# Block 1 of a chunked linear attention in 64-token chunks, spread between parts of the projection before it

## The chip, the cores and the metric

One Trainium2 chip, one core of it. The metric is the device time of one execution in microseconds; lower is better. The kernel takes float32 inputs and gives float32; inside it works in bf16 with float32 sums.

## The reference

An attention with decay (lightning attention) is followed by a gated feed-forward layer. B = 4 batches, H = 8 heads, S = 768 tokens, D = 64; the model width is 512 and d_ff is 1536.

```python
for b in range(nb):                       # blocks of 64 tokens
    intra = einsum('bhic,bhjc->bhij', qb, kb) * Dmask      # lam ** (i - j), i >= j
    intra = einsum('bhij,bhjd->bhid', intra, vb)
    inter = einsum('bhid,bhde->bhie', qb * lam_pow, kv_state)
    out[:, :, sl] = intra + inter
    kv_state = lam_block * kv_state + einsum('bhsd,bhse->bhde', kb * rev_pow, vb)
...
x = out, as (B * S) x 512
result = (sigmoid(x @ w_gate) * (x @ w_val)) @ w_out
```

The length at which the tokens are cut into pieces is free as long as decays and states follow it: a piece of 128 tokens gives the same result as two of 64.

## The kernel before, in words

The 768 tokens are walked in six blocks n = 0 to 5 of C = 128 tokens, for all 4 batches and 8 heads at once; so a block is 512 rows of the feed-forward layer. For each block there are three stages.

1. Attention. q and k are transposed so that the head dimension lies on the partitions (`QS`, `KS`), two heads on the 128 partitions; q is multiplied by the decay table `lamq`. Scores (`sp`) are masked into `MT`, outputs (`op`) are summed from the state (inter: `ST` times `QS`) and from the scores (intra: `v` times `MT`) and copied to `XT`, and the state of the next block is made (`cp`, from the decayed keys `KD`, then an update into `ST`).
2. `piece_gv` (L566): for each of 12 slices `ft` of d_ff four matmuls with WG into `gp`, four with WV into `vp` (each of 512 columns, in `product`, L556 to L561); ACT makes the tanh of gp (`sg`), DVE multiplies it with vp into `ht`.
3. `piece_po` (L592): for each batch `tt` twelve matmuls with WO into `po`, then a copy to `ob` and a store.

What sets the order is a list, `plan`, written by hand: units of stage 2 or 3, each with work of the next block's attention that is issued right behind it. Every engine does its instructions in the order in which they are issued. [...]

The blocks differ. Block 0 has a form of its own (`t_0`, `s_0`, `a_0`, `c_0`), in which tokens are laid in pairs; TensorE first multiplies zeros (`zeros`, L613) while loads are under way. Blocks from `FIRST_XBAR` = 2 on take q and k transposed by DMA and work in chunks of L = 64 tokens: `chunk_s`, `chunk_m`, `chunk_i`, `chunk_a`, `chunk_x`, `chunk_c`, with matmuls of 64 x 64 that stand four at a time in the quadrants of the array; the state between the two chunks is made by `update_0` (L533, from the decayed state `XD` of `decayed`), the one for the next block by `update_1` (L540). `in_order` (L505) makes TensorE wait until a named matmul has finished[...]; it stands between inter and intra outputs. For half of the batches (2 and 3) heads, and in the chunk form also the halves of the token rows of k and v, are swapped when loaded (`load`, L89).

Block 1 lies between the two. Its q and k are transposed by TensorE (`trans`, L706, `t_`, L280: matmuls of 128 x 128), and it works in one piece of 128 tokens: `piece_s` (L380), `piece_m`, `piece_i` (L398), `piece_a` (L410), `piece_x`, `piece_c` (L433). It needs tables of its own (`block_tables` L249, `block_mask` L262) and `chunk_lamq` (L259), which turns the query table into the chunk form once block 1 is done. In the plan (L763 to L770) its work lies behind parts of block 0's projection `po`, cut into first and second halves of six matmuls: transposes of batches 0 and 1 behind the second unit, their scores behind the third, transposes of batches 2 and 3 behind the sixth, scores behind the seventh, and `att(1)`, that is outputs, XT and states together, behind the last.

```python
order = [(gp, WG, whole), (vp, WV, whole)]
if ft == 0 and n <= 1:
    order = [(gp, WG, first), (vp, WV, first), (gp, WG, second), (vp, WV, second)][1 - n:]
```

These lines (L571 to L573) cut the first unit of blocks 0 and 1 into halves by batches, so that it can begin when XT holds batches 0 and 1.

## Time and profile before

| what | value |
|---|---|
| median of 3 runs | 223.56 us (223.34 to 223.59) |
| the profiled execution's own time | 223.48 us |
| its span, first to last instruction | 221.7 us |
| TensorE matmuls (PE) busy | 214.0 us, 97% |
| VectorE (DVE), ScalarE (ACT) busy | 104.6 us, 107.9 us |
| four matmuls of gp or vp, 512 columns | 0.86 us |
| DVE copy of one bank of XT, block 1 | two in 1.29 us |
| DVE update_0, one bank (L536) | 0.68 us |
| ACT copy of one bank of XT (L510) | 0.60 us |

The page gives each engine's busy time, then the span in 40 slices of 5.5 us with the busy share of each in tenths, then the chain of work that ended last: from the last instruction back to what released it. The timeline lists instructions in order of time, with the idle time of the engine ahead of each and what ended it in brackets. [...]

### The profile page before, as it was taken

How to read it: one execution, taken by the hardware profiler on the slowest of the kernel's cores; microseconds unless marked ns; L12 is line 12 of the kernel's file. 1: busy time of each engine (PE TensorE's matmuls, PEld its weight loads, DVE VectorE, ACT ScalarE, POOL GpSimd, SP SyncE). 2: the span in 40 equal slices, each digit the busy share in tenths (PEclk: the TensorE clock that was granted, in tenths of full speed). 3: DMA queues.
4: the chain of work that ended last, by engine and by line, in shares of the span. 5: the costliest groups of instructions: out<-in, count | busy, mean ns of one | idle time of the engine just before them, and what ended most of it. 6: DMA issues, size and time to landing. Idle time of an engine off the chain costs nothing.

```text
span 221.7 us, 5479 instructions
## 1 busy us (share of the span) xinstructions
PE 214.0 (97%) x2299; PEld 107.5 (48%) x2310; DVE 104.6 (47%) x192; ACT 107.9 (49%) x236; POOL 72.9 (33%) x101
## 2 busy tenths in 40 slices
PE   7689999999999999999999999999999999999994
PEld 2564444557445454454544444544445544444443
DVE  4854575539757430749420659430649400333301
ACT  5748764594393243773433683342592342333221
POOL 7999855760296009800970050000000000000000
PEclk9999999999999999999999999999999999999999
DMA  5999999999999999999999993012100012100022
GB/s 115 176 179 187 195 200 181 168 156 155 152 98 168 236 235 128 176 185 113 88 151 197 234 75 24 3 50 95 47 0 3 3 50 95 47 1 0 3 96 95
DMA packets 99657, 25.27 MB, mean 114 GB/s; under 512 B 90288, under 2 KB 96688, under 8 KB 99632
## 3 DMA queue, kind: packets, MB, share of 16 engines
q0 software_dynamic: 78128, 13.90, 78.3%
q1 hardware_dynamic: 20688, 10.69, 20.0%
q10 hardware_dynamic: 816, 0.33, 0.6%
q8 instruction: 18, 0.29, 0.5%
q14 instruction: 7, 0.06, 0.1%
HBM read 28.32 MB, written 6.29 MB: 156 GB/s over the span
## 4 chain that ended last, share of the span: by engine, by line
PE 92%; POOL 2%; DMA 2%; issue 1%; ACT 1%; POOLq 0%
PE gp L559 28%; PE po L599 28%; PE vp L559 28%; DMA vb<-in_v_dram 2%; PE sp L460 1%; PE op L498 1%; PE op L484 1%; POOL qb L119 1%; PE cp L521 1%; PE op L318 1%; POOL kb L119 1%; PE sp L386 0%; ACT XT L325 0%; PE op L417 0%; PE tq L284 0%
## 5 line engine op out<-in xcount | busy, mean ns | idle before, releaser
L554 DVE SCALAR_TENSOR_TENSOR ht<-sg,vp 128x512 bf16<-128x512 f32 x72 | 49.4, 686 | 84.4 <-PE vp L559 79.0
L559 PE MATMUL gp<-XT,WG 128*128 128x512 bf16 (+1 forms) x296 | 74.3, 373 | 0.5 <-ACT XT L325 0.5
L559 PE MATMUL vp<-XT,WV 128*128 128x512 bf16 (+1 forms) x296 | 74.3, 373 | 0.0
L577 ACT ACTIVATE sg<-gp 128x512 f32<-128x512 f32 x72 | 43.0, 597 | 57.0 <-PE gp L559 57.0
L599 PE MATMUL po<-WO,ht 128*128 128x512 bf16 (+2 forms) x291 | 63.4, 370 | 0.6 <-issue 0.2
L559 PEld LDWEIGHTS <-WV 128*128 128x128 bf16 x296 | 28.9, 98 | 33.3
L559 PEld LDWEIGHTS <-WG 128*128 128x128 bf16 x296 | 28.6, 98 | 32.6 <-issue 0.5
L599 PEld LDWEIGHTS <-ht 128*128 128x128 bf16 x300 | 28.3, 98 | 31.9
L603 ACT ACTIVATE ob<-po 128x512 f32<-128x512 f32 (+1 forms) x24 | 14.0, 583 | 40.4 <-PE po L599 40.4
L148 ACT ACTIVATE kd<-kb,kds 128x128 bf16<-128x128 bf16 x80 | 25.2, 391 | 0.0
L678 POOL COPY gates<-qt 128x1 bf16<-128x1 bf16 x4 | 1.4, 352 | 41.1 <-DMA qt<-qb 41.1
L107 POOL DMA_DIRECT2D kb<-in_k_dram x18 | 12.9, 768 | 2.6 <-DMA vb<-in_v_dram 1.6
L510 ACT CAST XT<-op 128x512 bf16<-128x512 f32 x16 | 8.2, 599 | 4.3 <-PE op L498 4.3
L470 DVE TENSOR_TENSOR MT<-sp,mask 128x512 bf16<-128x512 f32 x16 | 10.2, 682 | 0.0
L107 POOL DMA_DIRECT2D qb<-in_q_dram x10 | 8.9, 906 | 3.0 <-DMA WO<-in_moe_w_out_dram 3.0
L544 DVE SCALAR_TENSOR_TENSOR st<-st,pow_l,cp 128x128 bf16<-128x128 bf16 x24 | 6.5, 342 | 5.4 <-PE cp L521 5.4
L97 POOL DMA_DIRECT2D vb<-in_v_dram x6 | 6.9, 1151 | 2.8 <-issue 1.1
L126 POOL DMA_DIRECT2D WV<-in_moe_w_val_dram x9 | 7.5, 852 | 0.0
L123 POOL DMA_DIRECT2D WG<-in_moe_w_gate_dram x8 | 6.8, 851 | 0.0
L107 POOL DMA_DIRECT2D vb<-in_v_dram x8 | 6.6, 836 | 0.0
L97 POOL DMA_DIRECT2D kb<-in_k_dram x5 | 6.0, 1195 | 1.1 <-DMA WG<-in_moe_w_gate_dram 1.1
L616 PE MATMUL zps<-st 128*128 128x512 f32 (+1 forms) x8 | 4.6, 710 | 1.5 <-DVE st L179 1.5
(94 smaller groups left out, 132.9 us busy)
## 6 DMA issues: line engine op xcount, KB each, us to landing
out_dram<-ob SPq DMA_DIRECT2D x19, 256.0 KB, 2.1
qb<-in_q_dram POOLq DMA_DIRECT2D x14, 128.0 KB, 5.9
vb<-in_v_dram POOLq DMA_DIRECT2D x12, 128.0 KB, 4.5
WO<-in_moe_w_out_dram POOLq DMA_DIRECT2D x4, 384.0 KB, 12.6
vb<-in_v_dram POOLq DMA_DIRECT2D x6, 256.0 KB, 5.2
kb<-in_k_dram POOLq DMA_DIRECT2D x5, 256.0 KB, 8.8
qb<-in_q_dram POOLq DMA_DIRECT2D x5, 256.0 KB, 7.3
WG<-in_moe_w_gate_dram POOLq DMA_DIRECT2D x4, 256.0 KB, 6.9
```

Of the source, the lines that this page charges most:

```text
L97: nc.gpsimd.dma_start(out=T_[c, n][:, b0:nat], in_=src[b0:nat, :, sl, :].rearrange("b h s d -> s (b h) d"))
L107: nc.gpsimd.dma_start(out=T_[c, n][rows, m:b1, hs, :], in_=src[m:b1, hd, ts, :].rearrange("b h s d -> s (b h) d"))
L123: nc.gpsimd.dma_start(out=WG[:, :, f0 * 128:f1 * 128], in_=wg_r[:, :, f0 * 128:f1 * 128])
L126: nc.gpsimd.dma_start(out=WV[:, :, f0 * 128:f1 * 128], in_=wv_r[:, :, f0 * 128:f1 * 128])
L148: nc.scalar.mul(KD[n][:, at, i, :], T_["k", n][:, at, i, :], kds[:, min(n // FIRST_XBAR, 1), h:h + 1])
L470: nc.vector.tensor_tensor(out=MT[n, bp][:, u], in0=SP[n, bp][u], in1=mask[:, u ^ bp].unsqueeze(1).to_broadcast([128, 2, HP, L]), op=ALU.mult)
L510: nc.scalar.copy(XT[n][:, bp].rearrange("p m (j c i) -> p m j c i", j=2, c=2)[:, :, :, c, :], OP[n, c, bp])
L554: return nc.vector.scalar_tensor_tensor(out=o, in0=g, scalar=1.0, in1=x, op0=ALU.add, op1=ALU.mult)
L559: nc.tensor.matmul(ps[:, part], lhsT=W[:, mt, fs], rhs=XT[n][:, part, mt], start=(part is not second and mt == 0), stop=(part is not first ...
L577: nc.scalar.activation(sg, gp.rearrange("p a b -> p (a b)"), AF.Tanh, scale=0.5)
L599: nc.tensor.matmul(po[:, :c1 - c0], lhsT=HT[n, ft][:, tt * 128:(tt + 1) * 128], rhs=WO[:, ft, c0:c1], start=(ft == 0), stop=(ft == NFT - 1))
L603: (eng.mul if eng is nc.scalar else eng.tensor_scalar_mul)(o, po[:, :c1 - c0], 0.5)
```

## The change

Block 1 takes the chunk form. `piece_s`, `piece_m`, `piece_i`, `piece_a`, `piece_x`, `piece_c`, `block_tables`, `block_mask` and `chunk_lamq` go; k and v of block 1 are loaded with swapped row halves, as in later blocks (`turned`); the query table is made in the chunk form at once. Its work is spread: the transposes of batches 0 and 1 are done in quadrants, k and q side by side (`trans_quads`); the scores of batches 2 and 3 come with the inter outputs of chunk 0 (`scores_1`); states and intra outputs of chunk 0 behind three further projection matmuls (`chunk_0`); outputs of chunk 1 behind the last three (`chunk_1`); and the states of chunk 1 behind slice 2 of block 1's gate and value. Three evictions of `po` go from ACT to DVE. Six slices of block 1's gate and value are done in halves of 256 columns. In block 0, TensorE's zeros begin later and are fewer, the second half of v is loaded ahead of the first weights, and scores, transposes and outputs stand in another order.

```diff
-            turned = n >= FIRST_XBAR and c != "q"
+            turned = n > 0 and c != "q"
...
-                nc.scalar.mul(KD[n][:, at, i, :], T_["k", n][:, at, i, :], kds[:, min(n // FIRST_XBAR, 1), h:h + 1])
+                nc.scalar.mul(KD[n][:, at, i, :], T_["k", n][:, at, i, :], kds[:, h:h + 1])
...
     load0("v", 0, 2)
-    load_g(0, 1)
     load0("v", 2, 4)
-    load_v(0, 1)
-    for ft in range(1, 4):
+    for ft in range(4):
         load_gv(ft, ft + 1)
-    nc.gpsimd.iota(ip1, pattern=[[1, C]], base=1, channel_multiplier=0,
+    nc.gpsimd.iota(ip1, pattern=[[0, 2], [1, L]], base=1, channel_multiplier=0,
                    allow_small_or_imprecise_dtypes=True)
...
-    def chunk_x(n, c, bp):
-        nc.scalar.copy(XT[n][:, bp].rearrange("p m (j c i) -> p m j c i", j=2, c=2)[:, :, :, c, :],
-                       OP[n, c, bp])
+    def chunk_x(n, c, bp, eng=nc.scalar):
+        (eng.copy if eng is nc.scalar else eng.tensor_copy)(
+            XT[n][:, bp].rearrange("p m (j c i) -> p m j c i", j=2, c=2)[:, :, :, c, :], OP[n, c, bp])
...
             order = [(gp, WG, first), (vp, WV, first), (gp, WG, second), (vp, WV, second)][1 - n:]
+        elif n == 1 and 3 <= ft < 9:
+            order = [(ps, W, part) for ps, W in ((gp, WG), (vp, WV)) for part in (first, second)]
...
+    tc.add_manual_dep(nc.tensor.nop().ins, iota.ins.name, SYNC, reason="PE begins with the chain of the first block")
     zeros(2, FP32)
-    zeros(3)
...
-    zeros(1)
-    for b in range(2, 4):
-        t_0("q", b)
-        e_0("q", b, nc.scalar)
-    zeros(1)
+    t_0("q", 2)
+    e_0("q", 2, nc.scalar)
     s_0(2)
+    t_0("q", 3)
+    e_0("q", 3, nc.scalar)
     a_0(0, (nc.scalar,))
     a_0(1, (nc.scalar,))
     s_0(3)
-    zeros(1)
+    a_0(2, (nc.scalar,))
     new_gv(0, 0)
     product(0, 0, GV[0, 0][0], WG, first)
-    a_0(2, (nc.scalar,))
     a_0(3, (nc.scalar, nc.vector))
...
+    def trans_quads(n, bp):
+        def go():
+            bs = [2 * bp, 2 * bp + 1]
+            ps = {c: ps_at.tile([128, 2, HP, C], BF16, name="t" + c, tag="ps") for c in "kq"}
+            name = None
+            for phase in range(2):
+                if phase:
+                    in_order(name)
+                for i, b in enumerate(bs):
+                    for hp in range(HP):
+                        for u in range(2):
+                            for c, r in (("k", phase), ("q", 1 - phase)):
+                                name = nc.tensor.transpose(ps[c][rows_of(u), i, hp, chunk(r)],
+                                                           T_[c, n][rows_of(r), b, 2 * hp + u, :],
+                                                           ident[rows_of(r), chunk(r)]).ins.name
+            tks[n, bs[0]], tqs[n, bs[0]] = ps["k"], ps["q"]
+            e_k(n, bs)
+            e_q(n, bs)
+        return go
...
+    def scores_1():
+        chunk_s(1, 1)
+        new_xt(1)
+        for c, bp in A:
+            new_op(1, c, bp)
+        inner.append(chunk_i(1, A))
+        chunk_m(1, 1)
+
+    def chunk_0():
+        chunk_c(1, 0, (ps_ff, ps_ff))
+        for bp in range(2):
+            update_0(1, bp)
+        in_order(inner[0])
+        chunk_a(1, A)
+        for c, bp in A:
+            chunk_x(1, c, bp)
+
+    def chunk_1():
+        for c, bp in Z:
+            new_op(1, c, bp)
+        name = chunk_i(1, Z)
+        in_order(name)
+        chunk_a(1, Z)
+        for (c, bp), eng in zip(Z, (nc.vector, nc.scalar)):
+            chunk_x(1, c, bp, eng)
...
-    behind[5].extend([tables, block_tables])
+    behind[5].append(tables)
...
     for u in range(2):
-        behind[7 + u].append(do(block_mask, u))
-        behind[9 + u].append(do(chunk_mask, u))
+        behind[8 + u].append(do(chunk_mask, u))
...
-    po(0, 0, fts=lo)
-    po(0, 1, trans(1, 0), fts=lo)
-    po(0, 2, pair(piece_s, 1, 0), m_(1, 0), m_(1, 1), kd(1, 0, 4, parts=[0]), fts=lo)
-    po(0, 0, kd(1, 4, 8, parts=[0]), fts=hi)
-    po(0, 1, fts=hi)
-    po(0, 2, trans(1, 1), fts=hi)
-    po(0, 3, kd(1, 0, 8, parts=[1]), pair(piece_s, 1, 1), m_(1, 2), m_(1, 3), fts=lo)
-    po(0, 3, att(1), fts=hi)
+    V = nc.vector
+    po(0, 0, do(decayed, 1), kd(1, 0, 4, parts=[0]), fts=lo)
+    po(0, 1, trans_quads(1, 0), fts=lo)
+    po(0, 2, kd(1, 4, 8, parts=[0]), do(chunk_s, 1, 0), do(chunk_m, 1, 0), fts=lo)
+    po(0, 0, kd(1, 0, 4, parts=[1]), eng=V, fts=hi)
+    po(0, 1, kd(1, 4, 8, parts=[1]), eng=V, fts=hi)
+    po(0, 2, trans(1, 1), eng=V, fts=hi)
+    po(0, 3, scores_1, fts=lo)
+    po(0, 3, chunk_0, fts=hi[:3])
+    po(0, 3, chunk_1, fts=hi[3:])
...
-            more[2 * late].append(do(decayed, nx))
+            more[3 * late].append(do(decayed, nx))
...
         if n == 1:
-            more[0].append(chunk_lamq)
+            more[2].append(do(chunk_c, 1, 1, (ps_at, ps_at)))
+            for bp in range(2):
+                more[2].append(do(update_1, 1, bp))
             more[2].append(lambda: next_loads(2))
```

## The prediction

> **What bounds the kernel now.** I read the page's busy line, then the chain of work that ended last in order of time, then the timeline at the two places that the change touches.

> ```profile
> span 221.7 us, 5479 instructions
> ...
> PE 214.0 (97%) x2299; PEld 107.5 (48%) x2310; DVE 104.6 (47%) x192; ACT 107.9 (49%) x236; POOL 72.9 (33%) x101
> ...
> PE   7689999999999999999999999999999999999994
> ```

> TensorE is the bound: only the first three slices (to 16 us) and the very end hold real idle time. After 16 us each us of TensorE work or waiting is a us of time; DVE and ACT matter only where TensorE waits for a result of theirs. The chain in order of time (start, length, what) shows block 1's attention and, below, the same work of block 2, which runs in 64-token chunks already:

> ```profile
> 39.28 0.45 PE tk L284 x8
> ...
> 41.46 0.55 PE sp L386 x16
> ...
> 50.15 0.57 PE op L406 x32
> 50.72 1.01 PE op L417 x32
> 51.74 0.50 PE cp L439 x32
> 52.24 0.59 PE gp L559 x4
> ...
> 67.95 0.64 PE sp L460 x62
> 68.59 0.42 PE cp L521 x31
> ...
> 69.98 0.86 PE vp L559 x4
> ```

> From the end of block 0's state product (36.58) to block 1's first gate product (52.24) are 15.66 us. In it are 48 projection matmuls of 0.2158 us (a quarter of the 0.863 that four take in a gp or vp): 10.36. Attention with its switches costs the other 5.30: four transpose groups of 0.45, two of scores at 0.55, outputs 0.57 and 1.01, states 0.50 (4.97), and 0.33 between them. From block 2 I take the price of a 64x64 matmul, 0.010 us (0.64 for 64), and of an excursion into that form and back: 67.95 to the nominal start of gp, 69.98 - 0.863 = 69.12, is 1.17 us for 96 of them, 0.21 over; block 3 gives 0.17 at its scores (98.58 to 99.71) and 0.08 at its outputs (108.34 to 120.38, less 10.36 and 160 x 0.010).

> The timeline shows that block 1 starts just without a wait:

> ```profile
> 51.11 1.07 ACT L430 CAST XT<-op 128x512 bf16<-128x512 f32 x2 [0.32 <-PE op L417]
> ...
> 52.23 0.60 PE L559 MATMUL gp<-XT,WG 128*128 128x256 bf16 x4
> ```

> Outputs finish batch by batch; ACT copies the first two batches into XT until 52.18 while TensorE does the state products, and gp follows. The start of the program, in the same view:

> ```profile
> 7.58 0.79 POOL L123 DMA_DIRECT2D WG<-in_moe_w_gate_dram  x1
> 8.34 1.41 POOL L119 DMA_DIRECT2D vb<-in_v_dram  x2
> 9.69 0.82 POOL L126 DMA_DIRECT2D WV<-in_moe_w_val_dram  x1
> ...
> 15.34 0.61 PE L559 MATMUL vp<-XT,WV 128*128 128x256 bf16 x4
> 15.91 0.60 PE L559 MATMUL gp<-XT,WG 128*128 128x256 bf16 x4
> ```

> WV is issued at 9.69; the quickest of nine such loads lands after 5.7 us, so at 15.34 or later: the first vp starts when its weights come.

> [...] Here the four f32 records of zeros start 0.85 us apart from 1.53, and the bf16 zeros that follow are 0.22 us apart (weight loads at 4.90, two in 0.32)[...].

> **The change part by part.**

> *Start.* Gone are six bf16 zeros; the two f32 ones (four records, 3.41 us) begin after the iota at 3.46 instead of 1.53 and end near 6.9, where k's transposes began at 6.71. That 0.2 is hidden: the outputs wait for v until 12.0, and the DVE masks behind have 0.57 idle. v's second half moves ahead of WG's first piece by one issue (0.76): v lands near 13.45 instead of 14.2, WG near 14.2 instead of 13.45. Outputs of batch 2 run at 13.45; gp at 14.2, ending 14.63; batch 3, behind gp, meets its mask at 14.60 and ends 15.1; the copies take 0.42 (15.7). vp still waits for WV at 15.34, so the second gp starts at 15.77 instead of 15.91: -0.14. Bounds: -0.35 if WV isn't the last, +0.4 if WG lands 0.6 later, since batch 3 then stands behind gp.

> *Table work.* Nine DVE instructions go (six of block_tables, two block masks of 0.68, chunk_lamq), one decayed of 1.22 comes, after block 0's state product. DVE is idle beside all of them (79.0 us of its idle time ahead of ht end with vp's matmuls): 0. Without that cover ht would hold a PSUM bank and TensorE would wait by what DVE is late; it isn't near that here.

> *Loads.* k and v of block 1's upper batches come in row halves: two k issues and one v issue more, 0.7 us of POOL each, with the same bytes. POOL's waits (v at 36.43 waits for k, the last k2 pieces at 47.27 and 48.68 wait for block 1's v) say that transfers and not issue set the pace; so k lands near 43.8 and v near 48.7 as before. ACT's kd of those batches waits there (42.6 to 43.8); the other kd and the KS copy of batches 2, 3 queue behind, needed at 48.0 and ready near 47.5. First v use moves from 50.65 to 49.5. Hidden, 0.5 to 0.8 in hand; 1 us if v or k is 1.5 late. Block 2's q, k loads stand behind three more issues; its transposes have 5 us to spare.

> *Attention.* TensorE now does 64 transposes in quadrants, 64 scores, 128 outputs and 64 states in 64x64 form: 320 x 0.010 = 3.20, and trans(1,1) as before, 0.90. The build order shows six excursions (transposes, scores, scores with inner outputs, chunk 0, chunk 1, and the second states behind gv 2 of block 1). I take 0.13 each: 0.78 (ends 0.48 and 1.26). Two in_order waits stand directly behind what they wait for (between the transposes' phases, and in chunk 1); no trace row has one, and the nearest is a single 64x64 matmul's own 0.195 us: 0.20 each, 0.40 (0 to 0.6).

> *First new wait: chunk 1 for the state.* chunk_c(1,0) ends near 49.85. DVE then does two update_0 of 0.68 (L536) one after the other; with 0.17 for the matmuls to finish (most of the 0.195 us of a 64x64 record) and 0.05 for the signal (XT at 52.18, gp at 52.23) ST is whole 1.59 after that. TensorE has until then chunk 0's outputs (0.32 and the switch, 0.13) and three projection matmuls (0.65): 1.10. It waits 0.49 (0 to 0.8). Behind it: everything of TensorE. Before, nothing waited for a state within the block.

> *Second new wait: gp for XT.* chunk 1's outputs end, and gv(1,0) is TensorE's next instruction. The copies run on DVE and ACT side by side: 0.17 + 0.645 (L430 on DVE, two in 1.29) + 0.05 = 0.87 (0.6 to 1.0). The state products that covered it before are gone from here to behind gv 2. ACT's copy of (1,1) stands behind two XT copies and ob; it is due only at the second gp, 0.87 later: hidden.

> Evictions of po by DVE (three, about 0.68): between them DVE has QS and MT with 0.2 or more to spare: 0.

> *Halves.* Six gv units use 256 columns: eight matmuls more each, 48 x 0.0025 = +0.12[...]; the trace's 0.437 less 0.4315 a quarter agrees. update_1 (2.15 us of DVE) moves to gv 2 with decayed (1.22) behind it: ht 4 comes about 2 us late; the build lets vp 6, not gp 6, wait for it, which leaves 0.1: 0 (to +0.7).

> Sum: 3.20 + 0.90 + 0.78 + 0.40 + 0.49 + 0.87 = 6.64 against 5.30: +1.34; +0.12; -0.14: +1.32. The profiled execution took 223.48 with 221.7 of span; 223.48 + 1.32 = 224.8. The median is 223.56, 0.08 higher, within the spread of 0.25.

> **Rivals.**

> *Packing wins, no wait replaces it (faster).* Place: the last po of block 0. If switches cost the lower end (0.48) and in_order nothing, work is 4.58; with -0.14 + 0.12 the change is 4.56 - 5.30 = -0.74 plus the two waits. At 0.2 for both it is -0.54: 222.9. It decides at 0.3 of waiting together, where it passes below -0.45. For it: chunks are measured at 0.010 a matmul, and block 1's wide outputs took 1.01. Against: both waits follow from data that a DVE or ACT copy of 0.6 or more must deliver, with nothing issued between.

> *It cancels.* Waits of 0.75 together at middling switches (0.6) and drains (0.1): 4.80 + 0.75 + 0.12 - 0.14 - 5.30 = +0.23: 223.7. For it: the spread of switch prices. Against: the XT wait alone is 0.6 at least.

> *Cold or late.* With fewer zeros the array may be slow[...]; or v is 1.5 late, +1. With the forecast's sum about 226.0. For it: the zeros begin 2 us later. Against: from 6.9 to 15 TensorE is more than half busy, and transfers carry the same bytes.

> **How the numbers follow.** About 0.2% (0.45 us) is what a measurement of this kernel can tell from no change. Forecast, 224.8, own range 224.1 to 225.5: 0.66. Packing wins, 222.9: 0.14. Cancels, 223.7: 0.11. Cold or late, 226.0: 0.09. From the same cases: faster 0.14, same 0.12 (the cancelling case and a tail of the forecast), slower 0.74. The range 223.2 to 226.0 leaves out nearly all of the faster case and half of the late one, 0.18.

> **What would show it.** In the changed kernel's chain: TensorE waiting 0.3 to 0.8 for st from DVE ahead of the op matmuls of chunk 1, and 0.6 to 1.0 for XT ahead of block 1's first gp, that gp near 53.1 and an excursion of about 0.45 after gv 2; second gp of block 0 near 15.8; twelve half gp and vp units at 0.873. Wrong, if gp follows chunk 1 within 0.3, if TensorE idles for vb or kb in block 1, or if the matmuls at 16 us are at half speed.

## The result, and the profile after

The changed kernel takes 225.86 us (225.29 to 226.21, six runs), the kernel before 223.68 in the same comparison: a ratio of 1.0094, interval 1.0077 to 1.0112. The forecast was +1.32 us; +2.18 us came. The profiled executions differ by 2.3 us of span (221.7 and 224.0).

The page of the changed kernel, with the lines that answer to those of before, and the queue line that matters later:

```profile
span 224.0 us, 5911 instructions
...
PE 214.1 (96%) x2517; PEld 111.7 (50%) x2528; DVE 103.5 (46%) x184; ACT 107.0 (48%) x234; POOL 73.5 (33%) x104
...
PE   3989999997999999999999999999999999999994
...
q8 instruction: 20, 0.33, 0.6%
```

TensorE's busy time has hardly moved (214.0 to 214.1) and the span has grown by 2.3: what was added is waiting, not work. The row of tenths says where: a 7 in the tenth slice (50 to 56 us), where before there was a 9. The chain in order of time shows that stretch (start, length, what):

```profile
40.09 0.21 PE tk L624
...
41.93 0.54 PE sp L372 x32
...
48.65 0.38 PE sp L372 x32
49.03 0.29 PE op L396 x31
...
50.07 0.27 PE cp L433 x18
50.35 0.17 issue
50.52 0.36 PE cp L433 x14
50.87 1.29 DVE st L448 x2
52.20 0.48 PE op L396 x31
52.73 0.48 PE op L410 x32
53.23 0.70 DVE XT L422
53.98 0.61 PE gp L471 x4
...
55.46 0.33 PE vp L471 x3
55.79 0.10 issue
55.89 0.27 PE vp L471
```

Both forecast waits are there: for `st` ahead of chunk 1's outputs, and for XT ahead of gp. There are also two small pieces called "issue", one within the 32 matmuls of a state product and one within four matmuls of a vp. There TensorE waits for nothing that the page names.

Set out by landmarks (end of the record before, to after): end of block 0's state product 36.58 to 36.93, +0.35; from there to block 1's first gp 15.66 to 17.05, +1.39; from there to the end 169.46 to 170.02, +0.56. The stretch of +1.39 was forecast at +0.89 (the sum's 6.64 less 5.30, less the 0.45 of the states behind slice 2, which lie after it). Item by item, from the chain: transposes in quadrants 0.95, scores 0.64 and 0.77, transposes of 128 0.89, chunk 0 1.13, the switch ahead of chunk 1 0.08, wait for `st` 0.42, chunk 1 0.85, wait for XT 0.93: 6.66, where the same items were forecast at 6.19. The outliers are the first scores (0.64 for 0.45) and chunk 0 (1.13 for 0.77), and chunk 0 holds the first "issue" piece.

### The profile page after: what moved, and what is told of

Its sections match the earlier page's. It is cut to its first block, busy times and chain, and to the rows that moved or that the text cites. A ratio compares the mean times of both kernels' runs of the same rounds, so it can differ in the third digit from the quotient of the medians.

```text
span 224.0 us, 5911 instructions
## 1 busy us (share of the span) xinstructions
PE 214.1 (96%) x2517; PEld 111.7 (50%) x2528; DVE 103.5 (46%) x184; ACT 107.0 (48%) x234; POOL 73.5 (33%) x104
## 4 chain that ended last, share of the span: by engine, by line
PE 95%; DVE 1%; issue 1%; POOL 1%; ACT 1%; POOLq 0%
PE vp L471 28%; PE gp L471 28%; PE po L513 28%; PE zps L530 2%; PE sp L372 2%; PE op L396 1%; PE cp L433 1%; PE op L410 1%; PE tk L271 1%; PE sp L281 1%; PE op L297 1%; DVE st L448 1%; DVE MT L288 1%; PE tq L271 1%; POOL qb L120 1%
## 5 line engine op out<-in xcount | busy, mean ns | idle before, releaser
L471 PEld LDWEIGHTS <-WV 128*128 128x128 bf16 x320 | 31.2, 98 | 31.0
L471 PEld LDWEIGHTS <-WG 128*128 128x128 bf16 x320 | 30.8, 98 | 31.0 <-DVE XT L422 0.9
L517 ACT ACTIVATE ob<-po 128x512 f32<-128x512 f32 (+1 forms) x21 | 12.2, 583 | 38.3 <-PE po L513 38.3
L108 POOL DMA_DIRECT2D kb<-in_k_dram x20 | 13.9, 747 | 3.7 <-DMA WO<-in_moe_w_out_dram 2.5
L382 DVE TENSOR_TENSOR MT<-sp,mask 128x512 bf16<-128x512 f32 x20 | 12.8, 683 | 2.0 <-PE sp L372 2.0
L456 DVE SCALAR_TENSOR_TENSOR st<-st,pow_l,cp 128x128 bf16<-128x128 bf16 x32 | 8.6, 343 | 5.3 <-PE cp L433 5.3
L108 POOL DMA_DIRECT2D vb<-in_v_dram x10 | 8.2, 833 | 1.4 <-DMA WO<-in_moe_w_out_dram 1.4
L517 DVE TENSOR_SCALAR ob<-po 128x512 f32<-128x512 f32 (+1 forms) x4 | 2.6, 658 | 10.4 <-PE po L513 10.4
L448 DVE TENSOR_TENSOR st<-xd,cp 128x512 bf16<-128x512 f32 x10 | 6.7, 683 | 1.5 <-PE cp L433 1.5
L530 PE MATMUL zps<-st 128*128 128x512 f32 x4 | 3.8, 1090 | 3.6 <-POOL dij L183 3.6
```

The source lines that it names most:

```text
L108: nc.gpsimd.dma_start(out=T_[c, n][rows, m:b1, hs, :], in_=src[m:b1, hd, ts, :].rearrange("b h s d -> s (b h) d"))
L382: nc.vector.tensor_tensor(out=MT[n, bp][:, u], in0=SP[n, bp][u], in1=mask[:, u ^ bp].unsqueeze(1).to_broadcast([128, 2, HP, L]), op=ALU.mult)
L448: nc.vector.tensor_tensor(out=ST[n, 1][:, bp].rearrange("p h j d -> p h (j d)"), in0=XD[n][:, bp * HP:(bp + 1) * HP], in1=CP[n, 0][bp].rea ...
L456: nc.vector.scalar_tensor_tensor(out=ST[n + 1, 0][:, bp, hp], in0=ST[n, 1][:, bp, hp], scalar=dec_l[:, bp, hp:hp + 1], in1=CP[n, 1][bp][:, ...
L471: nc.tensor.matmul(ps[:, part], lhsT=W[:, mt, fs], rhs=XT[n][:, part, mt], start=(part is not second and mt == 0), stop=(part is not first ...
L517: (eng.mul if eng is nc.scalar else eng.tensor_scalar_mul)(o, po[:, :c1 - c0], 0.5)
```

## The experiments

Ratios are to the kernel before, which ran on the same chip each time. Kernels called "after" are the changed kernel with the edit shown.

**The zeros.** In the changed kernel they begin early again:

```diff
-    tc.add_manual_dep(nc.tensor.nop().ins, iota.ins.name, SYNC, reason="PE begins with the chain of the first block")
     zeros(2, FP32)
+    zeros(3)
```

> The changed kernel with the zeros of block 0 begun at once after the memset and five instead of two at the start, as before the change; all else as changed. Theory (slow array clock): k's first transposes run at 0.22 us per eight instead of 0.43, the second gp of block 0 starts at 15.77 instead of 16.26, and the whole is 0.4 to 0.5 us shorter than the changed kernel, near 225.4. Rival (the new order of block 0 or the later WG load costs it): the second gp stays near 16.26 and the time near 225.9.

225.75 us, 1.0099 [1.0084, 1.0114]: no gain. And the kernel before with late zeros (the opposite edit, without `zeros(3)`):

> The kernel before with only the late and fewer zeros of the change; loads and order of block 0 stay. Theory (slow array clock): transposes at 0.43 per eight, TensorE's dense stream starts 0.3 to 0.6 us later (second gp of block 0 at 16.2 to 16.5 instead of 15.91), the time near 224.1. Rival (the order costs it): second gp at 15.9 to 16.0, time 223.7.

223.56 us, 0.9995 [0.9985, 1.0004]: no cost. In both, the first vp waits for WV, whose load is on the chain for 6.08 and 6.31 us. Transposes at half speed until 9.4 us are visible in the changed kernel's trace (rows of eight start 0.43 us apart, from 7.29; in the kernel before, with its early zeros, 0.22), at a granted clock of 1.00, but WV hides them. With early zeros in the changed kernel a gap of 0.51 stands in the second vp of block 1's first slice, where the changed kernel has 0.10.

**The order of block 0 and of its loads**, alone in the kernel before:

```diff
-    load_g(0, 1)
     load0("v", 2, 4)
-    load_v(0, 1)
-    for ft in range(1, 4):
+    for ft in range(4):
...
-    zeros(1)
-    for b in range(2, 4):
-        t_0("q", b)
-        e_0("q", b, nc.scalar)
-    zeros(1)
+    t_0("q", 2)
+    e_0("q", 2, nc.scalar)
     s_0(2)
+    t_0("q", 3)
+    e_0("q", 3, nc.scalar)
...
-    zeros(1)
+    a_0(2, (nc.scalar,))
     new_gv(0, 0)
     product(0, 0, GV[0, 0][0], WG, first)
-    a_0(2, (nc.scalar,))
```

> The kernel before with only the new order of loads, scores, transposes and outputs in block 0; its early zeros stay, the three single ones between go. Theory: the dense stream starts 0.1 to 0.2 earlier (second gp of block 0 at 15.75 instead of 15.91), the time 223.5, hardly to be told from 223.7. Rival (batch 3 behind gp and the later WG cost time): second gp at 16.1 to 16.3, time 224.0.

223.51 us, 0.9999 [0.9987, 1.001]. Neither the forecast gain of 0.14 nor a loss. The start of the profiled execution (+0.35) is within what executions differ by: the second gp of block 0 began between 15.58 and 16.39 us in all the traces.

**The states of chunk 1 moved into the XT wait**, which they should fill:

```diff
             chunk_x(1, c, bp, eng)
+        chunk_c(1, 1, (ps_at, ps_at))
+        for bp in range(2):
+            update_1(1, bp)
...
-            more[2].append(do(chunk_c, 1, 1, (ps_at, ps_at)))
-            for bp in range(2):
-                more[2].append(do(update_1, 1, bp))
```

> The changed kernel with the states of chunk 1 and their updates right behind chunk 1, ahead of block 1's first gp, instead of behind slice 2. Theory (the wait for XT is idle time that other work can fill): the wait of 0.93 between the last output matmul and gp holds the 0.32 of state products, gp starts at the same 53.98, and the excursion behind slice 2 (0.49) is gone: 0.5 us shorter than the changed kernel, near 225.4. Rival (the time between is taken by the change of tiling form and not by the copy): gp starts 0.3 to 0.45 later and the sum stays within 0.1 of the changed kernel.

229.0 us (227.24 to 229.85), 1.0229 [1.0197, 1.0261]: 3 us worse than the changed kernel. Its chain:

```profile
52.81 0.13 PE cp L433 x14
52.94 2.87 issue
55.81 0.43 PE cp L433 x16
```

The states begin at once in the wait, and in the middle of them TensorE stands for 2.87 us, with no wait that the profile knows. This broke my theory that data waits make up the loss.

**What that gap is.** I counted TensorE's instructions in program order (weight loads, matmuls, waits): 4628 in the kernel before, 5066 after. The two "issue" pieces of the changed kernel lie 256 instructions apart, at positions 1212 and 1468. If the step is fixed, they set the positions for every kernel: 188 + 256k. Below, a *place* is an instruction at such a position; it should be felt wherever it falls among matmuls in quadrants. The other kernels test this. The queue called "instruction" moves 20 packets after and, on the page of before, 18:

```profile
q8 instruction: 18, 0.29, 0.5%
```

**The halves of slices 3 to 8**, out of the changed kernel (two lines), then into the kernel before:

```diff
-        elif n == 1 and 3 <= ft < 9:
-            order = [(ps, W, part) for ps, W in ((gp, WG), (vp, WV)) for part in (first, second)]
```

> The changed kernel without the halves of six slices in block 1 (96 TensorE instructions fewer). Theory A (only the fixed 2.5 ns of each matmul): 0.12 us shorter, near 225.75. Theory B (at every 256th TensorE instruction the engine runs dry for 0.1 to 0.3 us when 64x64 matmuls are around it, and the halves shift these places): the places then fall into scores, outputs and states of blocks 2 and later, each such stage is 0.1 to 0.2 longer, and the time is the same as or up to 0.6 longer than the changed kernel's, 225.8 to 226.4.

235.5 us, 1.0528 [1.0496, 1.056]. Taking out 96 instructions cost 9.6 us; theory B had expected 0.6 at most. The chain:

```profile
80.71 0.25 PE cp L433 x26
80.96 2.90 issue
83.86 0.23 PE cp L433 x5
...
114.95 0.22 PE cp L433 x22
115.16 4.24 issue
119.41 0.26 PE cp L433 x9
```

The counted places fall at instruction 55 and 47 of the 64 of the states (a weight load and a matmul for each of 32 products), that is behind 27 and 23 matmuls. The timeline has 27 and 23 before the gaps (the chain leaves one out each time). The count also says why: the outputs and states of one block are 128 + 128 + 64 = 320 instructions in 2.2 us. If a place falls in their first 64, a second falls in the states, too soon after it. The 96 instructions of the halves move the places of block 2 and later out of that window. The same two lines in the kernel before should then do harm:

> The kernel before with the change's halves alone: six slices of block 1 in 256 columns, 96 TensorE instructions more. Theory B (the instruction places, 256 apart): two places now fall into one run of 320 instructions of 64x64 form, in blocks 2, 3 and 4, the first in the inter outputs, the second in the state products after 22, 18 and 2 of 32; at the second TensorE is dry for 2.5 to 4.5 us each, and the time is 231 to 235. Rival (halves cost 2.5 ns a matmul and no more): 223.8, no gap.

230.48 us (229.35 to 232.22), 1.0322 [1.0281, 1.0363], against 223.41 before. They were to cost 48 x 0.0025 = 0.12 us. The timeline:

```profile
78.25 0.39 PE L521 MATMUL cp<-vb,kd 64*64 64x64 bf16 x22
81.51 0.28 PE L521 MATMUL cp<-vb,kd 64*64 64x64 bf16 x10 [2.87 <-issue]
...
116.75 0.39 PE L521 MATMUL cp<-vb,kd 64*64 64x64 bf16 x14 [2.23 <-issue]
...
151.96 0.50 PE L521 MATMUL cp<-vb,kd 64*64 64x64 bf16 x32
```

(Rows overlap: in this form one matmul's record is 0.195 us long, and the starts are about 0.01 us apart.) Both gaps are where the count puts them (45 and 37 of 64: behind 22 and 18). A third was expected and didn't come, and the time is below the 231 to 235 expected: the third block has its 32 states in 0.50, without a gap, though its places lie as close. The windows of this kernel say what differs (span, busy time of PE, PEld, DVE, ACT, POOL with counts, granted clock, DMA share, GB/s):

```profile
78.00:81.50 3.50, 0.64 (x53) 0.49 (x41) 0.00 (x0) 2.05 (x4) 0.08 (x1) 1.00 1.16 171
81.50:85.00 3.50, 3.49 (x20) 1.43 (x20) 2.15 (x8) 0.00 (x0) 1.58 (x4) 0.67 0.52 150
85.00:88.50 3.50, 3.50 (x15) 1.53 (x14) 0.00 (x0) 0.60 (x1) 3.50 (x5) 0.84 1.65 106
...
150.50:153.00 2.50, 2.50 (x165) 1.84 (x164) 1.14 (x3) 1.25 (x4) 0.00 (x0) 1.00 0.00 0
```

The last row has no DMA traffic, the first 171 GB/s. (In the kernel without halves the same block has 5 GB/s, and its place in the states cost 0.18.) And after the gap the granted clock is down: over the 7 us from 81.5 it is short by (0.33 + 0.16) x 3.5 = 1.7 us of full speed. So in this execution each gap costs its length and about 1.7 more: 2.87 + 2.23 + 3.4 = 8.5, and it is 8.7 above that of before (230.4 and 221.7 of span). It is the slowest of six. The three that had a mean clock of 0.998 or more took 229.35 to 229.73: the lower clock follows in some executions only.

**The places shifted** by 48 instructions with halves in three slices of block 0:

```diff
-        elif n == 1 and 3 <= ft < 9:
+        elif n == 1 and 3 <= ft < 9 or n == 0 and 3 <= ft < 6:
```

> The changed kernel with three slices of block 0 in halves as well: 48 TensorE instructions more ahead of block 1, and 24 matmuls more at 2.5 ns, 0.06 us. Theory B (gaps at every 256th instruction): the gap of 0.17 inside the state products of chunk 0 and that of 0.26 in the second vp of block 1's first slice vanish; gaps come at 59 of 64 instructions of the inner outputs behind the scores and at 47 of 64 of chunk 1's outputs; the time within 0.2 of the changed kernel. Rival (the gaps belong to what is waited for there: loads, PSUM banks, weights): they stay where they are, in the state products and in the second vp.

229.97 us, 1.0279 [1.0251, 1.0308]: 4 us more than the changed kernel, where 0.2 at most was expected. The count puts a place at 47 of the 64 instructions of chunk 1's intra outputs, behind 23 matmuls:

```profile
52.43 0.38 PE op L410 x23
52.80 2.15 issue
54.95 0.32 PE op L410 x9
```

The two gaps of the changed kernel are gone, as theory B has it. At the other new place, 59 of the inner outputs, no gap shows. This edit touches no instruction of block 1, nor what one waits for. It moves the places, and the loss comes with them.

**The state earlier**, so that chunk 1 needn't wait for it:

```diff
+        chunk_c(1, 0, (ps_ff, ps_ff))
         inner.append(chunk_i(1, A))
         chunk_m(1, 1)
-
-    def chunk_0():
-        chunk_c(1, 0, (ps_ff, ps_ff))
         for bp in range(2):
             update_0(1, bp)
+
+    def chunk_0():
```

> The changed kernel with the state products of chunk 0 one step earlier, behind the scores of batches 2 and 3 instead of behind the next three projection matmuls; the updates behind the masks on DVE. Theory (outputs of chunk 1 wait for two DVE updates in a row): the wait of 0.29 for st is gone, and about 0.1 of switching; 0.3 to 0.4 us shorter than the changed kernel, near 225.5. Rival (v lands too late, or DVE's masks then stand in the way): a wait for vb or for MT takes its place and the time stays within 0.1.

225.95 us, 1.0109 [1.0091, 1.0127]. The wait for `st` is gone, and its time isn't won:

```profile
48.86 0.20 PE op L396 x21
49.06 1.42 issue
50.48 0.28 PE op L396 x11
```

The count gives instruction 43 of the inner outputs, behind 21. TensorE resumes at 50.48, as in the changed kernel (50.52).

**A later cut of `po`**, two and four matmuls instead of three and three, for the same wait:

```diff
-    po(0, 3, chunk_0, fts=hi[:3])
-    po(0, 3, chunk_1, fts=hi[3:])
+    po(0, 3, chunk_0, fts=hi[:2])
+    po(0, 3, chunk_1, fts=hi[2:])
```

> The changed kernel with the six last projection matmuls of block 0 cut two and four instead of three and three around chunk 0, so that the states are one matmul earlier and one more matmul stands ahead of chunk 1. Theory (chunk 1 waits for two updates on DVE in a row): the wait for st of 0.29 between the last projection matmul and chunk 1 falls to 0 or nearly, 0.25 to 0.3 lower, near 225.6. Rival (masks of batches 2 and 3 then come late, or the wait is the form's): the wait moves to MT or stays, time near 225.9.

225.57 us, 1.0089 [1.0069, 1.0108]. Its timeline:

```profile
50.54 0.29 PE L433 MATMUL cp<-vb,kd 64*64 64x64 bf16 x13 [0.70 <-issue]
50.66 0.45 PE L410 MATMUL op<-MT,vb 64*64 64x64 bf16 x32
51.05 1.04 PE L513 MATMUL po<-WO,ht 128*128 128x512 bf16 x4
52.01 0.65 PE L396 MATMUL op<-QS,st 64*64 64x64 bf16 x32
```

The states reach their place half a us sooner, the gap is 0.70 instead of 0.17, and they resume at 50.54: what was gained ahead of the place was lost at it.

**Each XT copy of chunk 1 halved** between DVE and ACT:

```diff
-        for (c, bp), eng in zip(Z, (nc.vector, nc.scalar)):
-            chunk_x(1, c, bp, eng)
+        for c, bp in Z:
+            for m, eng in ((slice(0, 2), nc.vector), (slice(2, 4), nc.scalar)):
+                (eng.copy if eng is nc.scalar else eng.tensor_copy)(
+                    XT[1][:, bp].rearrange("p m (j c i) -> p m j c i", j=2, c=2)[:, m, :, c, :], OP[1, c, bp][:, m])
```

> The changed kernel with each copy of chunk 1's outputs into XT cut in two, one half on DVE and one on ACT, so that the batches that the first gp takes are whole after half a copy; TensorE's instructions stay the same. Theory (gp waits for the copy): its start comes 0.25 to 0.3 earlier relative to chunk 1's outputs, and the time is 0.25 lower, near 225.6. Rival (the time between is the change of tiling form): gp stays 0.9 behind.

225.79 us, 1.0104 [1.0085, 1.0123]. In the trace gp follows the start of the last outputs by 0.99 us instead of 1.25, as meant; the timing can't tell that from nothing. This execution passes the place in the states of chunk 0 near 49.6 without a gap. So the length at one place differs between executions of the same TensorE instructions. Its next place, in the first slice's second vp, shows 0.24.

**Both last edits together:**

> The changed kernel with both: copies into XT cut in two and projection matmuls two and four. Theory: the two gains add, 0.5 to 0.6 lower than the changed kernel, near 225.3, still 1.6 above the kernel before: switching, drains, the late states of chunk 1 (0.49), the halves (0.12) and the instruction places stay. Rival (the waits are the whole loss): 223.7 to 224.2.

225.54 us, 1.0091 [1.007, 1.0111]; the gap in the states is 0.48 and ends at 50.45. So four kernels (50.52, 50.48, 50.54, 50.45) resume within 0.1 us of each other, though they reach the place between 49.06 and 50.35. **All of it** (early zeros, states in the XT wait, the state early, no halves):

> The changed kernel with early zeros, states of chunk 1 as filler ahead of gp, states of chunk 0 earlier and no halves. Theory: the single gains add up: 0.45 + 0.5 + 0.35 + 0.1 less what the 256-instruction places take back (0 to 0.5): 1.0 to 1.4 shorter than the changed kernel, 224.5 to 224.9, still 0.8 to 1.2 above the kernel before, since the wait for XT (0.6 left) and the switches stay. Rival (chunk form is the shorter one once its waits are covered): at or below 223.6.

235.44 us, 1.053 [1.0504, 1.0555]. Each edit was meant to remove a wait of the changed kernel; together they put the places as badly as in the kernel without halves (the count gives instruction 26 of chunk 1's states in block 1 and 50 of the states in block 2). No version of the changed kernel beats the kernel before.

**When the refills land.** The traces keep each packet of the queue "instruction", 16 KB, with its start and length. With the states in the XT wait, the stretch from 53.4 to 54.4 us holds one (count, MB, share):

```profile
q8 instruction: 1, 0.02, 5.8%
```

Set beside the gaps (us from the start of the span; stops are those of the chains and timelines above):

| kernel | TensorE stops | refill starts, lands | TensorE resumes | after the landing |
|---|---|---|---|---|
| changed, states of chunk 0 | 50.35 | 48.17, 49.11 | 50.52 | 1.41 |
| changed, second vp of block 1 | 55.79 | 53.58, 54.52 | 55.89 | 1.37 |
| states in the XT wait | 52.94 | 53.46, 54.38 | 55.81 | 1.43 |
| no halves | 80.96 | 81.24, 82.38 | 83.86 | 1.48 |
| no halves | 115.16 | 117.17, 118.14 | 119.41 | 1.27 |
| places shifted | 52.80 | 52.59, 53.65 | 54.95 | 1.30 |
| state earlier | 49.06 | 48.16, 49.11 | 50.48 | 1.37 |
| XT copies halved, states of chunk 0 | no gap | 45.16, 46.09 | (49.64) | 3.55 |

In ten traces I find 26 such stops, and each ends 1.3 to 1.6 us after the one refill that landed between the place before and this one. So TensorE waits there for a refill. That is why removed waits brought nothing near 50 us: four kernels resume together because their refills land together (48.90 to 49.11). With the copies halved, TensorE has the same instructions, but in that execution the refill began 3 us sooner, and the gap is missing.

## Why the prediction was right, and where it was short

*Sign and mechanism: right; the size came out short.* The measured +2.18 is within the outer range, but 225.86 lies above the 224.1 to 225.5 that I gave the forecast itself, and nearest to the 226.0 of the rival "cold or late", whose slow array the zeros rule out (225.75 with early ones), and whose late v no chain shows. The two new waits are the ones named, at the places named, and about the size given: 0.42 for the forecast 0.49 (`st`), 0.93 for 0.87 (XT). That they are real waits shows in the early state (the wait goes) and the split copies (the wait shrinks by 0.26). Removing either didn't shorten the run by more than can be told. For the state the trace shows why: TensorE stood at a place ahead of chunk 1 instead. For XT, the place behind it took 0.24 where the changed kernel has 0.10; the rest isn't settled.

*In-order waits and transposes: right.* 0.95 for the forecast 0.97 in quadrants; 0.89 for 0.90; second scores with inner outputs 0.77 as forecast.

*"I take 0.13 each": the term that was too small.* Excursions were priced as a constant, from block 2 and block 3. The first scores and chunk 0 came 0.19 and 0.36 dearer. Both hold an instruction place (at 62 of 64, and 37 of 64), where TensorE waits for a refill: two weight loads stand 0.17 apart there in the scores (the second at 42.26, 1.38 after a landing) and 0.39 apart in the states (at 50.52), where their neighbours stand about 0.01 apart. The same chunk 0 without that stop, in the split-copy execution, took 0.89, about a quarter of a us less. Together the two exceed the whole 0.47 by which these items came dearer.

The price of 0.21 from block 2 of the kernel before holds something else as well. Its rows are

```profile
68.41 0.60 PE L521 MATMUL cp<-vb,kd 64*64 64x64 bf16 x32
...
77.35 0.95 PE L498 MATMUL op<-MT,vb 64*64 64x64 bf16 x64
```

where block 3 of the same kernel has 0.46 and 0.79 for them: a pause of some 0.15 in each. These pauses aren't refills. They lie about 6 and 108 instructions behind a place, 11.1 and 5.0 us after the last landing, and block 3's row of 0.46 holds a place too. In the kernel before with halves, where the places have moved by 96 instructions, they stay in their rows:

```profile
68.56 0.59 PE L521 MATMUL cp<-vb,kd 64*64 64x64 bf16 x32
...
77.49 0.94 PE L498 MATMUL op<-MT,vb 64*64 64x64 bf16 x64
```

So part of the 0.21 that I read as a switch was neither a switch nor supply. What it was stays open.

*The states behind slice 2: right*, 0.49 for 0.45. *Halves: right as a sum, wrong as a role.* Their own cost is 0.13 in the changed kernel: eleven rows of eight matmuls of 256 columns take 9.62 us (starts from 59.92 to 69.54), 0.8745 each, where four of 512 take 0.863; that is 2.8 ns for each of the 48 added. (The forecast's own numbers give that too: 0.437 less 0.4315 is for two more matmuls, 2.75 ns each.) "48 x 0.0025 = +0.12" misses that 96 more instructions decide where every later place falls: 9.6 us in favour of the changed kernel, 7.1 against the kernel before.

*After the first gp* +0.56 was measured and +0.57 forecast (0.45 + 0.12), partly by luck: 0.27 was lost at the place in the first slice, and about 0.2 came back because the two rows of block 2 above take 0.45 and 0.89 in the changed kernel.

*"-0.14" at the start: not borne out*, nor is the half-speed start a loss; the rival "cold or late" named a real effect (transposes at half speed to 9.4 us, 0.43 for 0.22) that lies behind WV's load. *Packing wins* and *cancels* are out: waits of 1.35 stood where they needed 0.3 and 0.75.

*Left open.* The traces have the refills but not what asks for them, so why some start late isn't shown. DMA traffic is likely: where two places fall into the chunk work of one block of tokens, the refill for the second starts 1.2 to 3.3 us after the first of them in the four blocks with traffic (kernel before with halves, changed kernel without), and about 1 us or more ahead of it in the two blocks with none or 5 GB/s. Of the +2.18 between medians, the stretch and what follows give 1.95 in one execution each; whether the rest is the start I can't tell, since the start's parts alone measured nothing.

## What to carry to other kernels

Where a tensor program turns to many small matmuls, count its instructions as well as its columns. Here 256 of them are 1.3 us in quadrants and 28 us in 512-column work. Two places in one run of 320 instructions stopped TensorE for 2.23 to 4.24 us in four blocks of tokens, while at the 15 places among 512-column matmuls in the traces of before and after no start is more than 0.216 us behind the last, their usual pace. Before trusting a move of such a stretch, mark every 256th instruction (the step found here), and look at what falls where and when the packets of the queue "instruction" land: here an edit meant to be free cost 4 to 10 us. When a removed wait brings nothing, look at whether the engine resumes at the same time as before, and at what holds it there.

## What the runs showed that I had not expected

- A place that comes 1 to 3 us after the one before it cost 2.15 to 4.24 us of standing still where DMA traffic ran (135 to 171 GB/s during the five stops whose windows I read), and nothing or 0.18 in the two blocks without (0 and 5 GB/s); behind the long stops TensorE resumed 3.6 to 5.7 us after the earlier place. At 50 us the place before lay in the scores near 42, yet the wait was 0.17 to 1.42, since the refill began only near 48. Where a refill had landed 2 us or more before, a place among matmuls in quadrants showed next to nothing (weight loads at most 0.03 us apart), but for one pause of 0.11 in the changed kernel, at 80.2, which I can't explain.
- In the 64 states of block 0, a place costs nothing visible (0.64 for 64 in both kernels); 20 us of 512-column work stand ahead of it.
- Behind stops of 2.23, 2.87 (two) and 4.24 us the granted clock was lower: 0.54, 0.67 and 0.50 over 3.5 us, and 0.78 over 7.6. Behind one of 1.42 and one of 2.90 it was 1.00. With the states in the XT wait the four first units of block 1, 256 columns each, run at 0.85 instead of 0.44; behind the stop of 2.15, with the places shifted, so do the three that follow the first. The windows behind the stop with the states in the XT wait, and behind the one of 2.90 in the kernel without halves, read (the clock is the third number from the end)

```profile
55.80:59.30 3.50, 3.49 (x32) 2.56 (x32) 2.15 (x8) 0.34 (x1) 0.00 (x0) 0.50 1.26 119
...
84.00:92.00 8.00, 8.00 (x42) 3.64 (x38) 2.15 (x8) 1.20 (x3) 6.56 (x8) 1.00 1.20 147
```

So TensorE was slower behind a stop of 2.15 us in one execution, and not behind one of 2.90 in another: the length of a stop alone doesn't decide it, and what else does isn't shown.
